# Linear attention's key sums on one core: two heads a product, four chunks a burst, and the denominators' sums by accumulating transfers

## The chip, the core and the metric

The kernel runs on one NeuronCore of a Trainium2 chip. The core has a matrix engine (TensorE, PE in the profile; its loads of stationary tiles are a row of their own, PEld), three elementwise engines (VectorE or DVE, ScalarE or ACT, GpSimd or POOL) and SyncE (SP), which issues most of the DMA transfers. The engines run their own instruction streams in order and wait for each other on semaphores. The metric is the device time of one execution in microseconds (us). Before the change it was 516.2 us, the median of three runs (515.8 to 516.62).

## What is computed

For 2048 tokens of width 512 the output is a gated mix of two layers, `g * a + (1 - g) * b`, with `g` the sigmoid of a dot product per token. `b` is a feed-forward layer of width 1792 with a squared ReLU. `a` is linear attention with 32 heads of 16 values each:

```python
pq = jnp.einsum("bhsd,hdf->bhsf", q, w_phi)
pk = jnp.einsum("bhsd,hdf->bhsf", k, w_phi)
phi_q = jnp.concatenate([_softmax(pq, axis=-1), _softmax(-pq, axis=-1)], axis=-1)
phi_k = jnp.concatenate([_softmax(pk, axis=-1), _softmax(-pk, axis=-1)], axis=-1)
kv = jnp.einsum("bhsf,bhsd->bhfd", phi_k, v)
z  = jnp.einsum("bhsf->bhf", phi_k)
num = jnp.einsum("bhqf,bhfd->bhqd", phi_q, kv)
den = jnp.einsum("bhqf,bhf->bhq", phi_q, z)[..., None] + 1e-6
o = num / den
```

All inputs are 32-bit floats. What the change touches are `kv`, for each head the sum over all tokens of the key features (32 numbers) times the values (16), and `z`, the sum over all tokens of the key features alone.

## The kernel before

**The feed-forward layer carries the order of the work.** A work list of 56 entries runs through two sweeps (one half of the 1792 hidden columns each), four blocks of 512 tokens and seven groups of 128 hidden columns. For each entry TensorE does 12 products "up" (into `u`) and 12 products "down" (into `d0` to `d3`); each 32-bit product is made of three, of high and low parts (`mm3`, lines 68 to 72). Between two entries stand slots: slot 2t comes ahead of entry t's up products and slot 2t+1 ahead of its down products. All attention work is placed by `at(slot, function, ...)` into these slots. The tile framework then orders each engine's instructions, with a priority for those under `tc.high_priority`.

**Keys and values** belong to the first sweep. The 16 chunks of 128 tokens follow each other 2.9 slots apart. `do_k` projects a chunk's keys into one bank of TensorE's accumulators, `exps` makes the two sets of exponentials from it (maxima, minima and two differences on DVE, lines 331 to 334; exponentials on ACT, line 336; sums and reciprocals on DVE), and `scaled` (line 345) multiplies them into the features `phi`, 1024 numbers per token. Two slots later `do_v` projects the values into the same single bank, and ACT copies them (line 517) into `vext`, whose rows have 17 numbers per head: 16 values and a one, written at the start by GpSimd. Five slots after the second of two chunks `do_kv` makes their products: for each head a stationary tile of 17 columns (values and the one) and 32 moving columns (the features), 32 products per chunk, 64 per burst, four different 32-column strips of the array one after the other (line 354). All chunks accumulate in one bank, `kvps`, in rows 32j to 32j+16 and 256 columns; row 16 of each strip holds `z`, because of the one.

**After the last chunk** (slot 53) `kv_done` copies the four strips to `kvs` (line 543), sends `z` through DRAM to all partitions (`zrow`, lines 546 and 549), transposes `kvs` on TensorE (`kvt`, line 554) and copies the result into `kvb`, which the numerators (`num`, line 400) use. GpSimd multiplies the query features with `z` (line 363).

**Beside that**, DVE folds the query weights with `w_phi` in 64 steps (`foldq_step`, line 236), each with a load of 256 KB (`wqr`, line 229, on SP's queue); after each 16 steps it transposes a quarter into `wqt`, and at slot 46 `foldq_move` writes all of it to DRAM (`wqm`) in four transfers and reads it back as the rows `wq`, which `foldq_ready` splits into high and low parts (`wqh`, `wql`).

Buffers are shared by tag: `e` and `ez` hold features (three in all), `phiT` is one large tile used in turn by several stages, `vz` holds `vext` and later `z`, `oh` and `ol` the numerators and until then the tokens of the gate (`gate_load`).

Of the kernel before, what the change touches and what calls it, by code (L numbers as in the profile page):

```python
# [26 lines left out]
VW = DH + 1  # L27
NV = 3
# [4 lines left out]
def tile_gated_mix(ctx: ExitStack, tc: tile.TileContext, xT, xn, wqT, wkT, wphi, wv, wo, w1, b1, w2, b2, gw, out):  # L33
# [110 lines left out]
    hold = pool("hold", NV)  # L144
# [15 lines left out]
    vext = [hold.tile([P, H * VW], F32, tag="vz", name=f"vext{i}") for i in range(NV)]  # L160
    heads = lambda v: v.rearrange("p (h v) -> p h v", v=VW)
    for v in vext:
        nc.gpsimd.memset(heads(v)[:, :, DH:VW], 1.0)
# [62 lines left out]
    def foldq_step(i):  # L226
# [10 lines left out]
        if e == DH - 1:  # L237
            if g == 0:
                st["wqt"] = work.tile([P, 2, 4, NG, 32], F32, tag="phiT", name="wqt", bufs=1).rearrange(
                    "p u r g s -> p (u r g s)").rearrange("p (c g j) -> p c g j", c=4 * NK, g=NK)  # L240
            nc.vector.transpose(st["wqt"][:, :, g, :], st["acc"].rearrange("p (c j) -> p c j", c=4 * NK))

    def foldq_move():
        for r in range(4):
            nc.sync.dma_start(wqm.rearrange("c i (r n) -> r i c n", r=4)[r],
                              st["wqt"][32 * r:32 * r + 32].rearrange("p c g j -> p c (g j)"))
        st["wq"] = [row() for _ in range(NK)]
        for k in range(NK):
            nc.sync.dma_start(st["wq"][k], wqm[4 * k:4 * k + 4].rearrange("c i n -> (c i) n"))
# [45 lines left out]
    def gate_load(n):  # L295
        t = st["xn", n] = work.tile([P, D], F32, tag="ol" if n % 2 else "oh", name="xn", bufs=2)
        nc.sync.dma_start(t, xn[n])
# [25 lines left out]
    def exps(ps, tag="e"):  # L323
# [4 lines left out]
        e = work.tile([P, H, 2, DH], F32, tag=tag, name="e", bufs=2 if tag == "e" else 1)  # L328
# [21 lines left out]
    def kv_chunk(n, kvps, phi, v):  # L350
        for i in range(NG):
            for j in range(4):
                h = 8 * (i % 4) + 4 * (i // 4) + j
                nc.tensor.matmul(kvps[32 * j:32 * j + VW, 32 * i:32 * i + 32], v[:, h * VW:(h + 1) * VW],
                                 phi[:, 32 * h:32 * h + 32],
                                 start=(n == 0 and i == 0), stop=(n == NB * NC - 1),
                                 skip_group_check=True)

# [149 lines left out]
    def do_k(b, c):  # L508

        n = b * NC + c  # L510
        e3, r = exps(project(c, st["x", b], st["wa"], "k"), "ez" if n % NV == NV - 1 else "e")
        st["phi", n] = scaled(e3, r, nc.vector)

    def do_v(b, n, c):
        ps = project(c, st["x", b], st["wb"], "v")
        with tc.high_priority(offset=AHEAD):
            nc.scalar.activation(heads(vext[n % NV])[:, :, :DH], ps.rearrange("p (h f) -> p h f", f=DH), AF.Copy)

    def do_kv(n):
        if n == 0:  # L520
            st["kv"] = ps_b.tile([P, 2 * P], F32, tag="s", name="kvps")
        for m in (n, n + 1):
            kv_chunk(m, st["kv"], st["phi", m], vext[m % NV])

# [12 lines left out]
    def kv_done():  # L537
        kvps, kvs = st["kv"], row()[:, :2 * P]
        nc.gpsimd.memset(kvs, 0.0)
        for j in range(4):  # L540
            s = slice(32 * j, 32 * j + VW)
            with tc.high_priority(offset=AHEAD):
                nc.vector.tensor_copy(kvs[s, :], kvps[s, :])
        zr = zrow.rearrange("(i q j f) -> q j i f", i=4, q=2, f=32)
        for q in range(2):
            nc.sync.dma_start(zr[q], kvs[DH::32, q * P:(q + 1) * P].rearrange("p (i f) -> p i f", f=32))
        for half in range(2):
            z = hold.tile([P, H * VW], F32, tag="vz", name=f"z{half}")[:, :D]
# [7 lines left out]
        for j in range(4):  # L556
            s = slice(32 * j, 32 * j + 32)
            with tc.high_priority(offset=AHEAD):
                nc.vector.tensor_copy(kvb[s, :, DH * (j % 2):DH * (j % 2 + 1)], kt[s, :, :DH])
# [35 lines left out]
    for b in range(NB):  # L595
        for c in range(NC):
            s = b * SL + 3 * c - 5 if b else 3
            at(s, gate_load, b * NC + c)
            at(s + 3 if b else 7 + c, gate_dot, b * NC + c)
# [139 lines left out]
```

## Time and profile before

| | |
|---|---|
| median of 3 runs | 516.2 us (515.8 to 516.62) |
| the profiled execution | 515.94 us |
| its span, first to last instruction | 514.2 us |
| PE busy | 509.1 us |
| DVE busy | 400.9 us |
| ACT busy | 227.0 us |
| POOL busy | 44.1 us |
| DMA | 75.35 MB, 147 GB/s on the mean |

A row of a group reads: line, engine, operation, output <- inputs (buffer numbers left out), shape and count, then times. A row of the timeline reads: start in us from the span's start, duration in us, engine, line, operation, count. A row of waits reads: who waited for whom, us in total, times, longest. PE's records of products overlap, because products are pipelined; the distance of their starts tells what one costs.

### The profile page before, as it was taken

To read this page: it belongs to the slowest core of one execution; us is meant where nothing else is said; L and a number is where in the kernel's file an instruction comes from. 1 tells how busy PE (TensorE), PEld (TensorE's weight loads), DVE (VectorE), ACT (ScalarE), POOL (GpSimd) and SP (SyncE) were. 2 spreads that over 40 slices of the span, in tenths; PEclk is the share of its full clock that TensorE was granted. 3 is DMA by queue.
4 is the path that set the end of the run, shared out by engine and by line. 5 is a ranking of instruction groups with operands and counts; after the bars stand their busy time and mean duration, and the time that the engine had idled before them with its cause. 6 is when DMAs were issued, how large, how long until landed. Compare 5 with 4: busy or idle time off the path is not lost.

```text
span 514.2 us, 9242 instructions
## 1 busy us (share of the span) xinstructions
PE 509.1 (99%) x3526; PEld 410.1 (80%) x3526; DVE 400.9 (78%) x680; ACT 227.0 (44%) x389; POOL 44.1 (9%) x44
## 2 busy tenths in 40 slices
PE   9999999999999999999999999999999999999997
PEld 4887888888888888888888878788787878788875
DVE  3769769796988798886889787988779677797723
ACT  5676253254224344253854544243625353343530
POOL 1000000000000000000003040301111111202100
PEclk9999999999999999999999999999999999999999
DMA  8997535467644477558359152213153321032102
GB/s 290 302 330 231 160 112 176 132 208 253 211 140 146 152 264 218 203 145 222 91 165 343 43 174 65 92 45 101 34 158 114 84 78 47 4 100 82 43 22 82
DMA packets 48421, 75.35 MB, mean 147 GB/s; under 512 B 7032, under 2 KB 15736, under 8 KB 48376
## 3 DMA queue, kind: packets, MB, share of 16 engines
q1 hardware_dynamic: 47912, 74.35, 45.8%
q8 instruction: 28, 0.46, 0.4%
q10 hardware_dynamic: 432, 0.39, 0.2%
q14 instruction: 17, 0.14, 0.1%
q0 software_dynamic: 32, 0.01, 0.0%
HBM read 50.60 MB, written 17.83 MB: 133 GB/s over the span
## 4 chain that ended last, share of the span: by engine, by line
PE 98%; ACT 1%; DVE 0%; DVEq 0%; issue 0%
PE u L70 10%; PE d L70 10%; PE u L72 10%; PE d L71 10%; PE d L72 10%; PE u L71 10%; PE v L70 3%; PE k L70 3%; PE k L71 3%; PE k L72 3%; PE q L72 3%; PE att L70 3%; PE q L70 3%; PE q L71 3%; PE att L71 3%; PE att L72 3%
## 5 line engine op out<-in xcount | busy, mean ns | idle before, releaser
L435 ACT ACTIVATE r<-u,b1c 128x512 f32<-128x512 f32 x56 | 38.6, 689 | 164.7 <-PE u L72 164.2
L70 PE MATMUL d<-w2h,hh 128*128 128x512 f32 x224 | 87.5, 391 | 0.0
L72 PE MATMUL d<-w2h,hl 128*128 128x512 f32 x224 | 87.3, 390 | 0.0
L71 PE MATMUL d<-w2l,hh 128*128 128x512 f32 x224 | 87.2, 389 | 0.0
L70 PE MATMUL u<-xh,w1h 128*128 128x512 f32 x220 | 86.6, 393 | 0.0
L72 PE MATMUL u<-xh,w1l 128*128 128x512 f32 x220 | 85.9, 390 | 0.0
L71 PE MATMUL u<-xl,w1h 128*128 128x512 f32 x220 | 85.7, 390 | 0.0
L65 DVE TENSOR_TENSOR hl<-r,hh 128x512 fp32r<-128x512 f32 x56 | 37.8, 675 | 35.5 <-ACT hh L62 35.5
L339 DVE TENSOR_REDUCE sm<-e 128x64 f32<-128x1024 f32 x32 | 38.9, 1216 | 28.2 <-ACT e L336 28.2
L363 POOL TENSOR_TENSOR ez<-e,z 128x512 f32<-128x512 f32 x32 | 42.0, 1332 | 217.6 <-ACT e L336 211.5
L70 PEld LDWEIGHTS u<-xh,w1h 128*128 128x128 f32 x220 | 41.3, 188 | 11.7 <-issue 2.1
L70 PEld LDWEIGHTS d<-w2h,hh 128*128 128x128 f32 x224 | 42.1, 188 | 9.3 <-issue 0.6
L72 PEld LDWEIGHTS d<-w2h,hl 128*128 128x128 f32 x224 | 42.1, 188 | 8.7
L71 PEld LDWEIGHTS d<-w2l,hh 128*128 128x128 f32 x224 | 42.1, 188 | 8.6
L72 PEld LDWEIGHTS u<-xh,w1l 128*128 128x128 f32 x220 | 41.3, 188 | 9.4 <-DVE w1l L65 0.8
L71 PEld LDWEIGHTS u<-xl,w1h 128*128 128x128 f32 x220 | 41.3, 188 | 8.3
L236 DVE SCALAR_TENSOR_TENSOR row<-wqr,phc,row 128x512 f32<-128x512 f32 x60 | 44.5, 741 | 3.9 <-DMA wqr<-in_wqT 3.5
L336 ACT ACTIVATE e<-e 128x1024 f32<-128x1024 f32 x32 | 33.8, 1057 | 22.7 <-DVE e L334 22.4
L387 ACT ACTIVATE phiT<-tb 32x256 f32<-32x256 f32 x64 | 26.4, 413 | 32.5 <-DVE tb L381 31.9
L62 ACT ACTIVATE hh<-r 128x512 fp32r<-128x512 f32 x56 | 35.3, 630 | 1.5
L436 ACT ACTIVATE r<-r 128x512 f32<-128x512 f32 x56 | 35.2, 628 | 1.1
L365 DVE TENSOR_REDUCE dz<-ez 128x64 f32<-128x1024 f32 x16 | 19.3, 1207 | 9.5 <-POOL ez L363 9.4
(102 smaller groups left out, 860.5 us busy)
## 6 DMA issues: line engine op xcount, KB each, us to landing
wqr<-in_wqT SPq DMA_DIRECT2D x64, 256.0 KB
in<-in_w SPq DMA_DIRECT2D x24, 256.0 KB
phiT<-tb SPq DMA_DIRECT2D x192, 32.0 KB
xin<-in_xT SPq DMA_DIRECT2D x16, 256.0 KB
xn<-in_xn SPq DMA_DIRECT2D x16, 256.0 KB
xkept<-xh SPq DMA_DIRECT2D x16, 256.0 KB
xkept<-xl SPq DMA_DIRECT2D x16, 256.0 KB
part<-row SPq DMA_DIRECT2D x16, 256.0 KB
```

Source lines behind the costliest of these rows:

```text
L62: i = nc.scalar.activation(hi, src, AF.Copy)
L65: st["low"] = elo.tensor_tensor(lo, src, hi.bitcast(F32), ALU.subtract)
L70: nc.tensor.matmul(o, ah[:, sa], bh[:, sb], start=first, stop=False)
L71: nc.tensor.matmul(o, ah[:, sa], bl[:, sb], start=False, stop=False)
L72: return nc.tensor.matmul(o, al[:, sa], bh[:, sb], start=False, stop=last)
L236: nc.vector.scalar_tensor_tensor(st["acc"], t, s, st["acc"], op0=ALU.mult, op1=ALU.add)
L336: nc.scalar.activation(ef, ef, AF.Exp)
L339: nc.vector.tensor_reduce(sm, e3, AX.X, ALU.add)
L363: nc.gpsimd.tensor_tensor(ez[:, hs, :], e3[:, hs, :], zbc[half], ALU.mult)
L387: nc.scalar.activation(dst, src, AF.Copy)
L435: nc.scalar.activation(r, ps, AF.Relu, bias=b1c[:, fc:fc + 1])
L436: nc.scalar.activation(r, r, AF.Square)
```

## The change

**Products.** The values are kept without the one, in 512 columns in another order (`val`), so that the values of two heads lie side by side as 32 columns. One product takes these as stationary tile and the features of the same two heads as 64 moving columns (two runs of 32). Of its result the two blocks on the diagonal are used; the other two are left alone. A chunk has 16 products in place of 32, and `do_kv` makes four chunks per burst in place of two: four bursts, in slots 18, 29, 41 and 53. Five buffers each for features and values replace three: two of the features' lie in `phiT` (`ebig`), two of the values' in the buffers of tag `ol`, so `gate_load` uses `oh` alone.

**The sums z.** GpSimd issues, after each of the first 15 chunks, a transfer of the features (128 x 1024 numbers) to `zacc` in DRAM, the first writing and the others adding to what stands there. SP loads the result (`zsum`) after chunk 15 has been scaled in the program's order. At the end of the last burst eight products with a stationary tile of ones (128 x 32) sum `zsum` and the features of chunk 15 over the partitions, into columns 256 to 511 of the same bank. `kv_done` copies the bank as a whole and sends one row of each strip to `zrow`.

**The folded query weights.** Each quarter is transposed into a row tile and written to `wqm` at once, in four transfers of 32 x 16 runs of 128 bytes; `wqt` is gone.

```diff
-NV = 3
+NV = 5
...
-    vext = [hold.tile([P, H * VW], F32, tag="vz", name=f"vext{i}") for i in range(NV)]
-    heads = lambda v: v.rearrange("p (h v) -> p h v", v=VW)
-    for v in vext:
-        nc.gpsimd.memset(heads(v)[:, :, DH:VW], 1.0)
+    zacc = dram.tile([P, 2 * D], F32, name="zacc")
+    val = [hold.tile([P, D], F32, tag="vz", name=f"val{i}") for i in range(3)]
+    val += [work.tile([P, D], F32, tag="ol", name=f"val{i}", bufs=2) for i in range(3, NV)]
...
-            nc.vector.transpose(st["wqt"][:, :, g, :], st["acc"].rearrange("p (c j) -> p c j", c=4 * NK))
...
+            t = row()
+            nc.vector.transpose(t, st["acc"])
+            for r in range(4):
+                nc.sync.dma_start(wqm.rearrange("c i (r g j) -> r g i c j", r=4, g=NK)[r, g],
+                                  t[32 * r:32 * r + 32].rearrange("p (c j) -> p c j", j=32))
...
     def kv_chunk(n, kvps, phi, v):
-        for i in range(NG):
+        ph = phi.rearrange("p (a g f) -> p a g f", a=4, f=2 * DH)
+        for i in range(4):
             for j in range(4):
-                h = 8 * (i % 4) + 4 * (i // 4) + j
-                nc.tensor.matmul(kvps[32 * j:32 * j + VW, 32 * i:32 * i + 32], v[:, h * VW:(h + 1) * VW],
-                                 phi[:, 32 * h:32 * h + 32],
+                m, g = i % 2, 4 * (i // 2) + j
+                nc.tensor.matmul(kvps[32 * j:32 * j + 32, 64 * i:64 * i + 64],
+                                 v[:, 64 * g + 32 * m:64 * g + 32 * m + 32], ph[:, 2 * m:2 * m + 2, g, :],
                                  start=(n == 0 and i == 0), stop=(n == NB * NC - 1),
                                  skip_group_check=True)
+    def z_keep(n):
+        nc.gpsimd.dma_start(zacc, st["phi", n], **({"accum_op": ALU.add} if n else {}))
+
+    def z_sum(kvps, parts):
+        one = nc.const_aps.tensor(1.0, (P, 32), F32)
+        for i, t in enumerate(parts):
+            for j in range(4):
+                nc.tensor.matmul(kvps[32 * j:32 * j + 32, 256:512], one, t[:, 256 * j:256 * j + 256],
+                                 start=i == 0, stop=i == len(parts) - 1, skip_group_check=True)
...
         st["phi", n] = scaled(e3, r, nc.vector)
+        if n < NB * NC - 1:
+            z_keep(n)
+        else:
+            st["z"] = work.tile([P, 2 * D], F32, tag="tb", name="zsum", bufs=2)
+            nc.sync.dma_start(st["z"], zacc)
...
-        for m in (n, n + 1):
-            kv_chunk(m, st["kv"], st["phi", m], vext[m % NV])
+        for m in range(n, n + 4):
+            kv_chunk(m, st["kv"], st["phi", m], val[m % NV])
+        if n == NB * NC - 4:
+            z_sum(st["kv"], (st["z"], st["phi", n + 3]))
...
-        kvps, kvs = st["kv"], row()[:, :2 * P]
-        nc.gpsimd.memset(kvs, 0.0)
-        for j in range(4):
-            s = slice(32 * j, 32 * j + VW)
-            with tc.high_priority(offset=AHEAD):
-                nc.vector.tensor_copy(kvs[s, :], kvps[s, :])
...
+        kvs = row()
+        with tc.high_priority(offset=AHEAD):
+            nc.vector.tensor_copy(kvs, st["kv"])
+        nc.sync.dma_start(zrow.rearrange("(j f) -> j f", j=4), kvs[::32, 256:512])
...
-            if c % 2:
-                at(s + 5, do_kv, n - 1)
+            if c == NC - 1:
+                at(s + 4.5, do_kv, n - 3)
```

How the instructions move is shown at three places. The first is TensorE's stream at the last burst, at the end of the first sweep; before the change:

```order
L354 MATMUL kvps<-e,vext_113 17x32 x32
L354 MATMUL kvps<-e,vext_111 17x32 x32
L70 MATMUL d_2491<-w2h_643,hh 128x512
L71 MATMUL d_2491<-w2l_644,hh 128x512
L72 MATMUL d_2491<-w2h_643,hl 128x512
L70 MATMUL d_2492<-w2h_643,hh 128x512
L71 MATMUL d_2492<-w2l_644,hh 128x512
L72 MATMUL d_2492<-w2h_643,hl 128x512
L70 MATMUL d_2493<-w2h_643,hh 128x512
L71 MATMUL d_2493<-w2l_644,hh 128x512
L554 MATMUL kvt<-ident,row 128x128 x2
```

And the same place after it, where line numbers are those of the changed file (L355 the products, L369 the ones, L580 the transposes):

```order
L355 MATMUL kvps<-e,val_114 32x64 x16
L355 MATMUL kvps<-ebig,val_115 32x64 x16
L355 MATMUL kvps<-ebig,val_116 32x64 x16
L355 MATMUL kvps<-e,val_112 32x64 x16
L369 MATMUL kvps<-zsum,const-float32-1.0 32x256 x4
L369 MATMUL kvps<-e,const-float32-1.0 32x256 x4
L69 MATMUL d_2323<-w2h_643,hh 128x512
L70 MATMUL d_2323<-w2l_644,hh 128x512
L71 MATMUL d_2323<-w2h_643,hl 128x512
L69 MATMUL d_2324<-w2h_643,hh 128x512
L580 MATMUL kvt<-ident,row 128x128 x2
```

The burst holds four chunks and the products of ones, and the transposes stand behind four products of the down group in place of eight.

The second is DVE's stream around the scaling of chunk 15 (the last row of each piece), with the splits of the folded query weights (`wql`); before:

```order
L339 TENSOR_REDUCE sm<-e 128x64
L65 TENSOR_TENSOR hl<-r,hh 128x512
L341 RECIPROCAL r<-sm 128x64
L303 SCALAR_TENSOR_TENSOR xn,lg<-xn,gwb 128x512
L345 TENSOR_TENSOR e<-e,r 128x1024
```

And after:

```order
L339 TENSOR_REDUCE sm<-e 128x64
L64 TENSOR_TENSOR wql_2633<-row,wqh_2632 128x512
L64 TENSOR_TENSOR wql_2675<-row,wqh_2674 128x512
L64 TENSOR_TENSOR wql_2691<-row,wqh_2690 128x512
L341 RECIPROCAL r<-sm 128x64
L64 TENSOR_TENSOR hl<-r,hh 128x512
L345 TENSOR_TENSOR e<-e,r 128x1024
```

Three splits, which stood behind the scaling, now stand ahead of it.

The third is DVE's stream at the copy of the finished sums; before:

```order
L65 TENSOR_TENSOR w2l_2932<-in,w2h_2931 128x512
L311 RECIPROCAL ge<-inv 128x1
L313 TENSOR_SCALAR eps<-inv 128x1
L65 TENSOR_TENSOR wol_3029<-in,woh_3028 128x512
L312 TENSOR_SCALAR rest<-ge 128x1
L543 COPY row<-kvps 17x256 x4
L65 TENSOR_TENSOR hl<-r,hh 128x512
L559 COPY kvb<-kvt 32x8x16 x4
```

And after:

```order
L64 TENSOR_TENSOR w2l_2703<-in,w2h_2702 128x512
L64 TENSOR_TENSOR wol_2808<-in,woh_2807 128x512
L64 TENSOR_TENSOR hl<-r,hh 128x512
L571 COPY row<-kvps 128x512
L64 TENSOR_TENSOR wol_2817<-in,woh_2816 128x512
L586 COPY kvb<-kvt 32x8x16 x4
```

The copy is one in place of four, and the split `hl` of the feed-forward layer moves from behind it to ahead of it.

On SP's queue the load of `zsum` stands behind the last four transfers to `wqm` and ahead of one load of `in` and the four loads `row<-wqm`; the first four loads of `x` for the second sweep move ahead of the loads of `wo`.

53 lines of the change are left out of this document (29 added, 24 removed).

## The prediction

> **What bounds the kernel now.** I read the page's busy row first, then the clock row, the chain that ended last and TensorE's waits.
>
> ```profile
> PE 509.1 (99%) x3526; PEld 410.1 (80%) x3526; DVE 400.9 (78%) x680; ACT 227.0 (44%) x389; POOL 44.1 (9%) x44
> PEclk9999999999999999999999999999999999999999
> PE 98%; ACT 1%; DVE 0%; DVEq 0%; issue 0%
> PE warm L467 <- DVE zeros L464: 1.2, 1, 1.2
> ```
>
> TensorE is busy for 99% of the span, its clock is granted in full, 98% of the chain lies on it, and its only listed wait is 1.2 us at the start. So the time is the sum of what TensorE spends from one product to the next. An edit counts in full if it changes that sum, and on other engines only if it makes TensorE wait.
>
> The sum has to be taken from starts, since busy times of overlapping products are unions. Here is TensorE's timeline around the first burst of keys-times-values products (`kvps`) and a normal stretch behind it; columns are start and duration in us.
>
> ```profile
> 61.08 0.39 PE L72 MATMUL d<-w2h,hl 128*128 128x512 f32 x1
> 61.40 1.27 PE L354 MATMUL kvps<-e,vext 128*17 128x32 f32 x128
> 62.59 0.50 PE L70 MATMUL v<-wvh,xh 128*128 128x512 f32 x1
> 65.44 0.39 PE L70 MATMUL u<-xh,w1h 128*128 128x512 f32 x1
> 68.16 0.39 PE L70 MATMUL k<-wkh,xh 128*128 128x512 f32 x1
> ```
>
> From 65.44 to 68.16 stand 12 ordinary products in 2.72 us: one per 0.2267. From 61.08 to 65.44 stand 13 such intervals (2.95) and the burst, 4.36 in all. **A burst costs 4.36 - 2.95 = 1.41 us.** How it splits shows in the counts of `kvps` records begun by 61.64, 61.90 and 62.40 (each 32-bit product leaves two records).
>
> ```profile
> L354 PE MATMUL kvps<-e,vext x32: 193/193/205, 61.4 to 61.6; 128*17 128x32 f32 x32
> L354 PE MATMUL kvps<-e,vext x60: 193/193/205, 61.4 to 61.9; 128*17 128x32 f32 x60
> L354 PE MATMUL kvps<-e,vext x120: 193/193/205, 61.4 to 62.4; 128*17 128x32 f32 x120
> L354 PE MATMUL kvps<-e,vext x1024: 190/193/207, 61.4 to 257.5; 128*17 128x32 f32 x171
> 256.38 1.32 PE L354 MATMUL kvps<-e,vext 128*17 128x32 f32 x128
> ```
>
> The first 32 come 7.5 ns apart (0.24 us), the rest 8.3 ns apart (60 in 0.50 us): 1.07 us for 128. The other 0.34 us is entering and leaving: the drain ahead of the burst and the slow products behind it. 1024 records are 8 bursts; the last is 0.05 longer (1.32 against 1.27). **All eight: 8 x 1.41 + 0.05 = 11.33 us.**
>
> **What a product of 64 columns takes.** The trace has none with a stationary tile of 32 columns over 128 rows. The nearest is `num` (32 columns stationary, 256 moving, eight tiles of the array abreast). These are its records begun by 304.73, 304.74, 305.16 and 305.17, and then the timeline.
>
> ```profile
> L400 PE MATMUL num<-phiT,kvb x8: 400/400/401, 304.5 to 304.5; 64*32 64x256 f32 x8
> L400 PE MATMUL num<-phiT,kvb x9: 376/400/401, 304.5 to 304.7; 64*32 64x256 f32 x9
> L400 PE MATMUL num<-phiT,kvb x24: 376/376/401, 304.5 to 305.0; 64*32 64x256 f32 x24
> L400 PE MATMUL num<-phiT,kvb x25: 376/376/401, 304.5 to 305.2; 64*32 64x256 f32 x25
> 304.18 0.39 PE L72 MATMUL d<-w2h,hl 128*128 128x512 f32 x1
> 304.50 1.09 PE L400 MATMUL num<-phiT,kvb 64*32 64x256 f32 x32
> 306.32 0.40 PE L70 MATMUL u<-xh,w1h 128*128 128x512 f32 x1
> ```
>
> Eight records start together and the next eight when these have passed: two groups in 0.43 us, 0.216 a group, 0.84 ns per column and tile. The moving side sets that pace. For 64 columns it gives 54 ns; `kvps` uses four tiles abreast, so 13.5 ns per record. The other end is twice the old pitch's first part, 15 ns, or twice its later part, 16.7. I take 14: the later 8.3 looks like a limit per instruction (a record brings a weight load and a product whatever its width), under which half as many records may each take 16.7 without feeling it.
>
> Four bursts of 128 records: 4 x (128 x 14 ns + 0.34) = 8.53 us, with ends 8.3 (13.5 ns) and 9.9 (16.7 ns). Against 11.33 this gains **2.80 us** (1.4 to 3.0).
>
> A rule would make it more. The Trainium skill, "TensorEngine Tiling (Array Packing)", Instruction Overhead, says that each matmul carries about 60 cycles of overhead, so that one column takes as long as 60; by it 64 columns would pass at almost the old 8.3 ns, and the gain would be 5.7 us in place of 2.8. The `num` rows speak against it at 256 columns, and no row here has 64; it stands among the rivals.
>
> **The products of ones** are new: eight at the end of the last burst, 256 columns each, 16 records, four abreast: 4 x 0.216 = 0.86 us. From 304.18 to 306.32 the `num` burst costs 2.14 less four intervals, 1.23, of which 0.86 are its four groups: 0.37 for entering and leaving, 0.03 more than the 0.34 already counted. Together **+0.89 us** (0.45 if eight could run abreast, 1.75 if two).
>
> **The accumulating transfers** (15, 512 KB each, on GpSimd's queue, each waiting for the one before) are shown by no row. GpSimd has nothing else queued behind them until the queries' products with `z`, so their price is lateness and DMA time.
>
> ```profile
> L345 DVE TENSOR_TENSOR e<-e,r x16: 1180/1217/1222, 38.7 to 247.4; 128x1024 f32<-128x1024 f32 x16
> q1 hardware_dynamic: 47912, 74.35, 45.8%
> b1c<-in_b POOLq DMA_DIRECT2D x1, 7.0 KB, 5.2
> 232.81 1.22 DVE L345 TENSOR_TENSOR e<-e,r 128x1024 f32<-128x1024 f32 x1
> 239.19 1.88 SPq L249 DMA_DIRECT2D row<-wqm  x4
> 260.87 0.39 PE L70 MATMUL q<-wqh,xh 128*128 128x512 f32 x1
> ```
>
> The features of a chunk are ready every (247.4 - 38.7) / 15 = 13.9 us. At the mean rate of q1 (45.8% of 514.2 us for 74.35 MB) 0.52 MB take 1.7 us; moved three times (read, read the sum, write) 5 us; GpSimd's one transfer needed 5.2 us to land with 7 KB. So my estimate lies between 1.7 and 10.3 us, under 13.9, and they do not pile up: 0 us. The skill's "DMA: Bandwidth & Descriptors", Anatomy of one DMA, fits 2.0 us plus bytes at 436 GB/s for this path, 3.2 us here; by it, too, nothing piles up.
>
> The load of the sums stands on SP's queue behind the last of them, and behind it wait `in` and the four `row<-wqm` loads of the queries' weights. The features of chunk 14 are ready at 234.0; with a transfer of 5 to 10 us the loads go out at about 242 to 247 instead of 239.2. The queries start at 260.87, 1.9 us earlier in the new program, and DVE now splits these weights ahead of scaling chunk 15. That scaling ends at 248.6 (247.4 + 1.22), and its burst starts at 256.38, 7.8 us later: three splits of 0.6 use 1.9, and 5.9 remain. A transfer up to about 12 us is covered; beyond that TensorE waits the excess.
>
> **The folding of the query weights** moves to 16 transfers of 128-byte runs from 4 of 512-byte runs, spread over 100 us, with the loads of `wqr` queued behind them on SP. Their cover is DVE's lead on TensorE, tightest in chunk 11.
>
> ```profile
> 186.58 0.67 DVE L334 TENSOR_TENSOR e<-mn,k 128x512 f32<-128x512 f32 x1
> 188.17 0.39 PE L70 MATMUL v<-wvh,xh 128*128 128x512 f32 x1
> DVE row L236 <- DMA wqr<-in_wqT: 3.5, 6, 1.0
> ```
>
> DVE frees the bank of `k` at 187.25, `v` takes it at 188.17: 0.9 us. Today DVE waits 3.5 us for `wqr` in 6 places, none of which reaches TensorE. With more DMA traffic I bound the new stalls between 0 and 3 us and take 0, since waits grow first where 2 to 4 us cover them.
>
> **The end of the sums** (kv_done): four copies become one, and the transposes `kvt` move up from behind eight products to behind four.
>
> ```profile
> 258.73 0.62 ACT L62 ACTIVATE hh<-r 128x512 fp32r<-128x512 f32 x1
> 257.82 1.72 DVE L543 COPY row<-kvps 17x256 f32<-17x256 f32 x4 [1.19 <-PE kvps L354]
> 259.58 0.69 DVE L65 TENSOR_TENSOR hl<-r,hh 128x512 fp32r<-128x512 f32 x1
> 259.69 0.41 PE L554 MATMUL kvt<-ident,row 128*128 128x128 f32 x2
> ```
>
> One copy of 128x512 takes about 0.7 us (as the `hl` row), 1.0 less than today, which is about what the four products fewer take away; but DVE now does `hl` first, which waits for ACT's `hh`. The last burst is longer by 1.6 us, so `hh` should be done by its end. Zero, at most 0.7 us. The larger load of the value copies, the new tiles for features and values, and the two gate buffers instead of four wait only for work several slots back: nothing.
>
> **Sum:** -2.80 + 0.89 = **-1.9 us**. The profiled execution took 515.94 us with a span of 514.2; that would be 514.0 and 512.3. The median shown is 516.2, 0.3 higher: **514.3 us**. One measurement of this kernel can tell about 0.2%, 1.0 us, from no change.
>
> **Rivals.**
> *The accumulating transfers pile up (slower).* Serial, each waiting for the last: from 39.9 (the first scaling's 38.7 and 1.2), 15 of length d end at 39.9 + 15d, and the sums must be read by about 255. It decides at d = 14 us. At 16 they end at 280, SP's queue and the last burst stand, and TensorE waits some 25 us: 539 us. For it: no row shows such a transfer, DMA is half busy. Against: it needs eight times the plain 1.7 us. Chance 0.08.
> *DVE comes late (no change).* The transfers and short runs delay `wqr`, DVE stands in front of the maxima of `k`, and `v` waits for the bank. With 2 us in all, 0.13 per chunk or a few of 0.5: 516.2. For it: the 0.9 us above. Against: 3.5 us of such waits cost nothing today. Chance 0.13.
> *The wider product takes twice the old later pitch* (16.7 ns, no gain per column): -1.4 + 0.9 = -0.5, 515.7 us, within the bound. Chance 0.06.
> *The count alone sets the time* (8.3 ns): -5.7 + 0.9 = -4.8, 511.4 us. Chance 0.05. The change then does more than the forecast; that its halving of the count brings nothing is the rival before.
>
> **How the numbers follow.** The forecast has 0.68; its own range is 513.2 (13.5 ns and ones at 0.45 give 513.6, less 0.4 for the scatter of the runs shown, 515.8 to 516.62) to 515.2 (1 us of small stalls). To hold 8 in 10 I go up to the second and third rival, 516.2 and a little scatter: **513.2 to 516.4**; the two outer ones, 0.13, and a little of the second, are left out. Faster by over 0.2%: 0.67 + 0.05 + 0.02 = 0.74. Within: 0.01 + 0.11 + 0.04 = 0.16. Slower: 0.08 + 0.02 = 0.10.
>
> **What would show it.** Right: four bursts, about 2.1 us each by the same sum of starts, the last near 3.0; records four at a time every 54 to 56 ns; `zacc` transfers landing within 10 us; no new wait of TensorE. Wrong: bursts of 1.4 us (count rules) or 2.5 us (16.7 ns); GpSimd's transfers back to back with no gap; a wait of TensorE's `v` for DVE, or of `kvps` for `zsum` or the scaling; `kvt` behind DVE's `hl`.

## The result and the profile after

The changed kernel takes **540.7 us** (median of 6 runs, 537.47 to 542.92) against 516.1 for the kernel before (6 runs, 515.76 to 516.83): ratio 1.047 [1.045, 1.050]. Forecast were 514.3 us and a range up to 516.4. The profiled execution took 542.42 us with a span of 540.6, 26.4 us more than before. The page of the changed kernel, the same rows as were shown of before, and the two DMA queues that carry the work (packets, MB, share of 16 engines' span):

```profile
PE 514.8 (95%) x3030; PEld 412.3 (76%) x3030; DVE 400.5 (74%) x677; ACT 227.3 (42%) x389; POOL 55.7 (10%) x55
PEclk9999999999799999999998999999999999999999
...
q1 hardware_dynamic: 54360, 74.87, 44.1%
q0 software_dynamic: 2192, 7.87, 8.5%
...
PE 68%; DMA 15%; DVE 11%; ACT 3%; issue 3%; SPq 0%; DVEq 0%; ACTq 0%
DMA wqr<-in_wqT 14%; PE d L70 7%; PE d L69 7%; PE d L71 7%; PE u L69 7%; PE u L71 7%; PE u L70 7%; PE q L71 3%; PE q L70 3%; PE att L70 3%; PE att L71 3%; PE att L69 3%; PE q L69 3%; DVE row L234 2%; PE num L413 2%
```

DVE has as much work as before (400.5 against 400.9 us), and TensorE is no longer the whole chain: its share went from 98% to 68%, and the largest single item is now a load, `wqr`, with 14%. The transfers to `zacc` are all but 0.01 MB of q0: 7.87 MB in 8.5% of the engines' time, where q1 moves 74.87 MB in 44.1%. Per byte that is 1.8 times as long.

First the part that was to gain. TensorE's timeline at the first burst and at the last, start and duration in us:

```profile
88.41 0.39 PE L71 MATMUL d<-w2h,hl 128*128 128x512 f32 x1
88.73 1.55 PE L355 MATMUL kvps<-e,val 128*32 128x64 f32 x96
90.09 0.63 PE L355 MATMUL kvps<-ebig,val 128*32 128x64 f32 x32
90.65 0.50 PE L69 MATMUL v<-wvh,xh 128*128 128x512 f32 x1
...
92.14 0.39 PE L69 MATMUL v<-wvh,xh 128*128 128x512 f32 x1
...
275.38 0.39 PE L71 MATMUL u<-xh,w1l 128*128 128x512 f32 x1
...
277.50 0.61 PE L369 MATMUL kvps<-zsum,const-float32-1.0 128*32 128x256 f32 x8
277.94 0.61 PE L369 MATMUL kvps<-e,const-float32-1.0 128*32 128x256 f32 x8
...
279.06 0.40 PE L71 MATMUL d<-w2h,hl 128*128 128x512 f32 x1
```

From 88.41 to 92.14 stand seven ordinary intervals (7 x 0.2267 = 1.59) and the burst: 3.73 - 1.59 = 2.14 us. From 275.38 to 279.06 stand three and the burst with the products of ones: 3.68 - 0.68 = 3.00. The two bursts between them cost 2.14 each by the same sum. Forecast were 8.53 / 4 = 2.13 and about 3.0. This part is as predicted to a few hundredths.

The loss stands in the waits: line, what it waited for, us in total, times, longest.

```profile
PE v L69 <- DVE e L334: 7.5, 3, 4.0
PE d L69 <- DVE row L716: 4.6, 1, 4.6
PE kvt L580 <- DVE row L571: 3.7, 1, 3.7
PE v L69 <- DVE ebig L334: 3.4, 2, 2.7
...
DVE row L234 <- DMA wqr<-in_wqT: 36.8, 20, 4.5
```

With two more rows, of 0.9 and 0.4, these are 20.5 us of TensorE's time, in nine places, eight of them behind DVE (the 0.9 is behind ACT); before there was none but the start. DVE's own wait for `wqr` grew from 3.5 to 36.8 us.

What happens in one of these places shows the timeline of the changed kernel from 124 to 140 us (SP's queue, GpSimd, DVE and TensorE, some rows left out):

```profile
124.58 0.64 SPq L227 DMA_DIRECT2D wqr<-in_wqT  x1
...
126.20 0.86 POOL L363 DMA_DIRECT2D zacc<-e  x1 [12.74 <-DVE eps L309]
...
126.50 4.22 SPq L227 DMA_DIRECT2D wqr<-in_wqT  x3
...
129.34 0.75 DVE L234 SCALAR_TENSOR_TENSOR row<-wqr,phc,row 128x512 f32<-128x512 f32 x1 [0.86 <-DMA wqr<-in_wqT]
...
134.06 0.39 PE L71 MATMUL u<-xh,w1l 128*128 128x512 f32 x1
...
135.18 0.75 DVE L234 SCALAR_TENSOR_TENSOR row<-wqr,phc,row 128x512 f32<-128x512 f32 x1 [4.48 <-DMA wqr<-in_wqT]
135.84 0.68 DVE L331 TENSOR_REDUCE mx<-k 128x32 f32<-128x512 f32 x1
...
137.64 0.68 DVE L334 TENSOR_TENSOR e<-mn,k 128x512 f32<-128x512 f32 x1
...
138.46 0.76 PE L69 MATMUL v<-wvh,xh 128*128 128x512 f32 x1 [4.01 <-DVE e L334]
139.03 0.63 PE L70 MATMUL v<-wvl,xh 128*128 128x512 f32 x1
139.45 0.63 PE L71 MATMUL v<-wvh,xl 128*128 128x512 f32 x1
139.88 0.63 PE L69 MATMUL v<-wvh,xh 128*128 128x512 f32 x1
```

Read it from the top. SP issues a load of `wqr` at 124.58; counted through, it is the 25th of 64, and the step at 135.18 is the 25th that needs one. GpSimd issues a transfer at 126.20, whose data move from 130.4 to 134.3 by the packet records of the trace. From 131 to 133 SP's queue then moves 45 GB/s, against some 195 in the four microseconds ahead of the transfer's data. So the load comes late though it was issued before the transfer; DVE, which works in order, stands 4.48 us in front of the step that needs it, and the maxima of `k` are queued behind that step; TensorE has the next `v` to do, whose bank is free only when DVE has read `k`, and waits 4.01 us. After the wait its products come 0.427 us apart, 139.03 to 139.88 in two steps, in place of 0.2267. The windows view (start and end, length, busy time and count of each engine, then granted clock, DMA share, GB/s) has the clock of that stretch:

```profile
140.00:144.00 4.00, 4.00 (x12) 3.14 (x11) 4.00 (x6) 1.51 (x4) 0.00 (x0) 0.56 0.79 289
```

0.56 of full speed is granted. So a wait of 4 us is paid about one and a half times: twelve products at 0.2 us more are 2.4. The same stands behind the two other waits of this length (4.6 and 3.7 us), and not behind those up to 2.7 us, where products follow at the ordinary pace. The Trainium skill, "TensorE: Matmul & The Clock Gate", Part 1, says that the array falls to half its clock after an idle window of about 3.4 us, with 426.7 ns from start to start at 512 columns; the 0.427 here agree.

The sum closes to about 1 us. From the starts of TensorE's products in the two traces, gaps over 0.7 us cost 21.9 us more than ordinary intervals after (0 before), and intervals of 0.3 to 0.7 us cost 9.9 us more, against 4.6 before: 27.2 in all. Span difference and forecast gain make 26.4 + 1.9 = 28.3.

### The profile page after: what moved, and what is told of

It is laid out like the page before. It is cut to its first block, busy times and chain, and to the rows that moved or that the text cites. A ratio compares the mean times of both kernels' runs of the same rounds, so it can differ in the third digit from the quotient of the medians.

```text
span 540.6 us, 8331 instructions
## 1 busy us (share of the span) xinstructions
PE 514.8 (95%) x3030; PEld 412.3 (76%) x3030; DVE 400.5 (74%) x677; ACT 227.3 (42%) x389; POOL 55.7 (10%) x55
## 3 DMA queue, kind: packets, MB, share of 16 engines
q1 hardware_dynamic: 54360, 74.87, 44.1%
q0 software_dynamic: 2192, 7.87, 8.5%
## 4 chain that ended last, share of the span: by engine, by line
PE 68%; DMA 15%; DVE 11%; ACT 3%; issue 3%; SPq 0%; DVEq 0%; ACTq 0%
DMA wqr<-in_wqT 14%; PE d L70 7%; PE d L69 7%; PE d L71 7%; PE u L69 7%; PE u L71 7%; PE u L70 7%; PE q L71 3%; PE q L70 3%; PE att L70 3%; PE att L71 3%; PE att L69 3%; PE q L69 3%; DVE row L234 2%; PE num L413 2%
## 5 line engine op out<-in xcount | busy, mean ns | idle before, releaser
L69 PE MATMUL d<-w2h,hh 128*128 128x512 f32 x224 | 88.9, 397 | 4.6 <-DVE row L716 4.6
L70 PE MATMUL d<-w2l,hh 128*128 128x512 f32 x224 | 88.6, 395 | 0.0
L234 DVE SCALAR_TENSOR_TENSOR row<-wqr,phc,row 128x512 f32<-128x512 f32 x60 | 44.7, 745 | 37.1 <-DMA wqr<-in_wqT 36.8
L339 DVE TENSOR_REDUCE sm<-e 128x64 f32<-128x1024 f32 x26 | 31.6, 1216 | 22.8 <-ACT e L336 22.8
L336 ACT ACTIVATE e<-e 128x1024 f32<-128x1024 f32 x26 | 27.5, 1058 | 34.8 <-DVE e L334 34.6
L400 ACT ACTIVATE phiT<-tb 32x256 f32<-32x256 f32 x64 | 26.5, 414 | 32.5 <-DVE tb L394 31.8
L69 PE MATMUL v<-wvh,xh 128*128 128x512 f32 x64 | 26.7, 417 | 11.3 <-DVE e L334 7.5
```

The lines of the kernel that those rows point to most:

```text
L69: nc.tensor.matmul(o, ah[:, sa], bh[:, sb], start=first, stop=False)
L70: nc.tensor.matmul(o, ah[:, sa], bl[:, sb], start=False, stop=False)
L234: nc.vector.scalar_tensor_tensor(st["acc"], t, s, st["acc"], op0=ALU.mult, op1=ALU.add)
L336: nc.scalar.activation(ef, ef, AF.Exp)
L339: nc.vector.tensor_reduce(sm, e3, AX.X, ALU.add)
L400: nc.scalar.activation(dst, src, AF.Copy)
```

## The experiments

Theory A: the transfers hold all DMA engines for some microseconds each, SP's loads behind them come late, DVE waits in lumps, TensorE waits for DVE, and the clock adds to it. Rivals: B, the 128-byte runs of the folded query weights on SP's queue are what delays the loads; C, the new order of the stream and the fewer buffers cost by themselves. "Wait for `wqr`" is DVE's, total and longest; "TensorE" adds up its listed waits without the 1.2 us at the start. Both are of the profiled execution, which for the plain transfers was the fastest of its four (525.3 us) and for `wqr` from 128 rows the slowest of its nine (522.6).

| run | time, us | ratio to before | wait for `wqr` | TensorE |
|---|---|---|---|---|
| before | 516.1 | | 3.5, 1.0 | 0 |
| changed | 540.7 | 1.047 [1.045, 1.050] | 36.8, 4.5 | 20.5 |
| one transfer | 515.3 | 0.999 [0.998, 1.000] | 11.1, 2.0 | 1.5 |
| before + short runs | 518.3 | 1.005 [1.003, 1.006] | 9.9, 2.2 | 2.5 |
| before + transfers | 531.9 | 1.032 [1.030, 1.035] | 27.9, 5.1 | 11.4 |
| plain transfers | 527.9 | 1.023 [1.019, 1.028] | 20.6, 3.8 | 8.4 |
| GpSimd adds | 525.1 | 1.017 [1.015, 1.020] | 7.7, 1.8 | 8.8 |
| 512-byte rows | 541.3 | 1.049 [1.047, 1.051] | 37.5, 4.5 | 19.1 |
| `wqr` from 128 rows | 520.1 | 1.007 [1.005, 1.010] | 2.9, 2.9 | 5.7 |
| every second transfer | 531.7 | 1.029 [1.026, 1.033] | 23.6, 5.2 | 11.2 |
| `zsum` by GpSimd | 535.2 | 1.037 [1.035, 1.039] | 33.5, 4.4 | 14.0 |
| both cures | 514.8 | 0.997 [0.996, 0.998] | 0.9, 0.9 | 1.5 |
| before + late DVE | 521.4 | 1.010 [1.008, 1.012] | 6.5, 1.9 | 4.3 |
| both cures, laid out | 514.5 | 0.997 [0.996, 0.998] | 2.5, 1.3 | 1.1 |

**One transfer.** All of the change, but `z_keep` for the first chunk alone:

```
-        if n < NB * NC - 1:
+        if n == 0:
             z_keep(n)
-        else:
+        elif n == NB * NC - 1:
```

> The changed kernel with only the first of its 15 transfers to zacc; the sums z are then those of chunks 0 and 15 alone. Theory A (each accumulating transfer holds all 16 DMA engines for 3 to 4 us, the wqr loads on SP's queue come late behind it, DVE waits for them ahead of the maxima of k, and TensorE waits for DVE): 514.2 us, between 513.4 and 515.2; DVE's wait for wqr falls from 36.8 to below 8 us, TensorE's listed waits from 21 to below 3 us. Theory B (the 128-byte runs of the folded query weights on SP's queue make wqr late): it stays above 530 us. Theory C (the new order of the streams and the fewer buffers make TensorE wait, whatever the DMA does): it stays above 530 us.

515.34 us. The order of the program, the buffers and the short runs are all in it, so B and C are out as main causes: 25 of the 26 us hang on 14 transfers. It is 1.1 us above A's point and just above A's range, and the wait for `wqr` is 11.1 us where A had below 8, most of it harmless.

**Short runs alone.** The kernel before, with the folded weights written a quarter at a time in 128-byte runs, as the change does:

```
-            nc.vector.transpose(st["wqt"][:, :, g, :], st["acc"].rearrange("p (c j) -> p c j", c=4 * NK))
+            t = row()
+            nc.vector.transpose(t, st["acc"])
+            for r in range(4):
+                nc.sync.dma_start(wqm.rearrange("c i (r g j) -> r g i c j", r=4, g=NK)[r, g],
+                                  t[32 * r:32 * r + 32].rearrange("p (c j) -> p c j", j=32))
```

> The kernel before with one part of the change alone: each quarter of the folded query weights is written at once in four transfers of 128-byte runs, in place of four transfers of 512-byte runs at the end. Theory A: 516.1 us, within 1 us. Theory B: over 528 us, with DVE waiting for wqr behind each quarter. Theory C: 516 us.

518.31 us: the short runs cost 2.3 us, more than the 1 us that A allowed, and far from B's 528.

**Transfers alone.** The kernel before, plus 15 accumulating transfers that nobody reads:

```
         st["phi", n] = scaled(e3, r, nc.vector)
+        if n < NB * NC - 1:
+            nc.gpsimd.dma_start(zacc, st["phi", n], **({"accum_op": ALU.add} if n else {}))
```

> The kernel before with 15 accumulating transfers of the features to DRAM added and nothing else changed; their result is not read. Theory A: 530 to 545 us, since the transfers alone carry the loss; DVE's wait for wqr rises from 3.5 to over 25 us. Theories B and C: 516 to 518 us.

531.89 us, with TensorE waiting 11.4 us in the same way: A's expectation. With the short runs that is 15.8 + 2.3 = 18.1 of the 24.6 + 1.9 = 26.5 us to be explained; some 8 were still open here.

**Plain transfers.** The changed kernel without the addition in the transfer:

```
-        nc.gpsimd.dma_start(zacc, st["phi", n], **({"accum_op": ALU.add} if n else {}))
+        nc.gpsimd.dma_start(zacc, st["phi", n])
```

> The changed kernel with plain transfers of the same features from the same queue in place of accumulating ones; z is then of chunks 14 and 15 alone. In the changed kernel a 4 KB packet of the accumulating queue took 383 ns on the mean, where a 2 KB packet of the plain queue took 100. Theory A: plain packets of 4 KB take about half as long, so a transfer holds the engines for under 2 us and the loss of 24 us falls below half: 515 to 526 us. Theories B and C, and a version of A in which any transfer of 512 KB on that queue is enough whatever it does: 536 to 543 us.

527.94 us, above A's range: a plain transfer of the same size harms half as much, and I had put its harm too low. The 536 to 543 of B, of C and of the version of A in which any transfer is enough are missed too. The row of its software queue stands against the 8.5% above:

```profile
q0 software_dynamic: 2192, 7.87, 3.9%
```

The same packets and bytes take 3.9% of 16 engines over 523.5 us, 327 engine-us for 15 transfers: 1.4 us of all 16 engines each. With the addition it is 8.5% over 540.6: 735 engine-us, 3.1 us of all engines each. This is the time that packets were under way, waiting for the other queue's packets perhaps included. DVE's wait for `wqr` goes the same way: over the run with one transfer, (20.6 - 11.1) / 14 = 0.7 us a transfer plain (in the fastest execution) and (36.8 - 11.1) / 14 = 1.8 with the addition.

**GpSimd adds.** No transfer; GpSimd adds the features on chip, bursts take three chunks:

```
-        nc.gpsimd.dma_start(zacc, st["phi", n], **({"accum_op": ALU.add} if n else {}))
+        if n == 0:
+            nc.gpsimd.tensor_copy(st["zacc"], st["phi", n])
+        else:
+            nc.gpsimd.tensor_tensor(st["zacc"], st["zacc"], st["phi", n], ALU.add)
```

> Keeps the wider products, but has no transfer to DRAM for the sums: GpSimd adds each chunk's key features into a tile of on-chip memory (the second half of the tile that held two more chunks' features), so a burst takes three chunks instead of four, the last one stands alone, and z_sum multiplies one tile by ones (4 products instead of 8). Nothing of the computation is left out. Theory A (the transfers hold the 16 DMA engines, SP's loads of wqr come late, DVE and then TensorE wait): the wait of DVE for wqr stays near the 11.1 us of the run with a single transfer, and the time is 514.0 to 516.5 us, ratio 0.996 to 1.001: products 16 x 2.12 = 33.9 against 45.3 us for eight bursts in the kernel before is what was already in the sum, less 0.5 for the ones, plus about 2.3 for the short runs. Rival C (the new order of the stream and the fewer buffers cost by themselves): with one buffer fewer it is 518 or more.

(The figures 33.9 and 45.3 in that expectation take a burst's cost for a chunk's; by the starts in this run's trace the six bursts with the ones cost 5 x 1.69 + 1.22 = 9.7 us, against 11.3 before.) 525.09 us: A's range is missed. C's 518 or more is met, but the trace shows another cause, so that this run says little on the fewer buffers. GpSimd's and DVE's groups, busy us and mean ns behind the bar, and then the same DVE steps with their shortest, median and longest ns:

```profile
L365 POOL TENSOR_TENSOR ebig<-ebig,e 128x1024 f32<-128x1024 f32 x11 | 29.4, 2674 | 135.3 <-DVE e L344 57.2 <-ACT val L544 26.9 <-DVE eps L308 26.8
...
L233 DVE SCALAR_TENSOR_TENSOR row<-wqr,phc,row 128x512 f32<-128x512 f32 x60 | 56.4, 940 | 8.4 <-DMA wqr<-in_wqT 7.7 <-DVE hl L64 0.3
L64 DVE TENSOR_TENSOR hl<-r,hh 128x512 fp32r<-128x512 f32 x56 | 43.4, 775 | 20.4 <-ACT hh L61 20.4
...
L233 DVE SCALAR_TENSOR_TENSOR row<-wqr,phc,row x60: 651/746/2775, 75.7 to 240.1; 128x512 f32<-128x512 f32 x60
```

The same DVE steps take 940 ns in place of 745 on the mean, and DVE's busy time goes from 400.5 to 428.5 us. The median is 746 all the same: six of the 60 steps, each under way during an addition of GpSimd, take 2.5 to 2.8 us, and the rest what they took before. So DVE is not slowed throughout; single instructions are held up for about 2 us each. `wqr` is on time (7.7), and yet TensorE waits 6.6 us for DVE and 2.2 for ACT. It is another way of making DVE late, with the same end.

**512-byte rows.** The transfers written as `p (c f)` with `f=128` on both sides.

> The changed kernel with each accumulating transfer written in rows of 512 bytes instead of 4096: the same bytes, eight times the packets. Theory A, with the two queues served packet by packet: SP's packets of 2048 bytes keep the larger share of each engine, wqr's wait falls from 36.8 us to 10 to 25, the time is 517 to 532. Rival (bytes read, added and written back are what holds the engines, or small packets cost the adder as much as large ones): wqr's wait stays at 35 or more and the time is 540 or more.

541.31 us, and this tells nothing: the software queue again shows 2192 packets and 7.87 MB, so the rows were joined again and the transfer was the same. Whether smaller packets would leave SP's loads more room stays open.

**`wqr` from 128 rows.** The transfers stay; the load reads 128 rows in place of 8 rows given 16 times:

```
-        nc.sync.dma_start(t, wqT.rearrange("(j e) g d -> g e j d", e=DH)[g, e].unsqueeze(1).to_broadcast([8, DH, D]))
+        nc.sync.dma_start(t, xn[i % (NB * NC)])
```

> The changed kernel, accumulating transfers included, but the 64 loads of wqr read 128 separate rows of xn (as many bytes, spread over all 16 DMA engines) in place of 8 rows of in_wqT, each repeated for 16 partitions, which use 8 of the 16 engines. The folded query weights come from the wrong numbers. Theory A: SP's queue now makes up its delay between two transfers at about twice the rate, DVE's wait for wqr falls from 36.8 us to under 12 and the time is 514.5 to 520. Rivals: the transfers harm through something other than wqr's loads (DVE's or TensorE's own pace, the order of the stream): 535 or more, whatever wqr waits; the loads are late because the transfers stop them altogether, not because they recover slowly: wait 25 to 37, time 530 to 541.

The query weights are then folded from other numbers; the bytes loaded and DVE's steps are the same. 520.13 us (517.05 to 522.56), 20.6 less than the changed kernel, with the median just above A's range, and DVE waits 2.9 us for `wqr`, once. So most of the transfers' harm does not reach DVE or TensorE directly; it goes through these loads, and what made the loads weak was their form. The windows view, first of the kernel before, at a place where four loads of `wqr` are on their way and nothing else (5 us x 199 GB/s are 1.0 MB), then of the last run below (rows separate), in a transfer and behind it; last two columns DMA share and GB/s:

```profile
213.00:218.00 5.00, 5.00 (x24) 4.14 (x23) 3.87 (x7) 2.82 (x4) 0.00 (x0) 1.00 0.54 199
```

```profile
206.00:208.00 2.00, 2.00 (x10) 1.68 (x9) 2.00 (x4) 0.00 (x0) 0.00 (x0) 1.00 1.03 228
209.00:215.00 6.00, 6.00 (x28) 4.99 (x27) 3.86 (x6) 2.66 (x4) 0.00 (x0) 1.00 1.03 391
```

With 8 rows given 16 times the queue moves 199 GB/s at a share of 0.54 and no more, though four loads are outstanding; with separate rows it goes, with the other writes and loads on it, at a share of 1.03 and 391 GB/s once the transfer (206 to 208) is through. The Trainium skill, "DMA: Bandwidth & Descriptors", Rules for kernel authors, says that an outermost dimension of size c below 16 confines a transfer to at most c engines; 8 of 16 fit the 0.54. The packet records agree: with nothing but these loads under way (before, 205 to 208 us) 7 to 10 packets are in flight at a time, in the last run (209 to 215) mostly 15 to 19, and a packet of 2048 bytes takes 84 ns in both (median). So it is half as many packets at once, and not slower ones from reading the same row again and again; which engines carry them the trace does not name.

These times also give an estimate of the harm. A packet of the accumulating transfer takes about 328 ns in 131 to 133. If an engine serves the two queues by turns, eight engines pass 8 x 2048 bytes of `wqr` in 328 + 84 ns, 40 GB/s; the 45 seen there are near it. That the engines take turns is argued from this, not shown.

**Every second transfer.** `z_keep(n)` for even `n` alone.

> The changed kernel with a transfer for every second chunk alone (chunks 0, 2, ... 14: 8 in place of 15, about 28 us apart in place of 14; the sums of the odd chunks but the last are left out). In the runs so far the time went up by about 1 us for each us that DVE waits for wqr beyond some 10 us. Theory A with a reserve that is refilled between transfers: wqr waits 10 to 20 us, time 514.5 to 521. Rival (each transfer costs the same, 26.4 us over 14): about 13 us over the run with one transfer, 526 to 530.

531.72 us, above both ranges: A's "reserve that is refilled in between" is refuted. DVE waits (23.6 - 11.1) / 7 = 1.8 us per transfer, as much as with twice as many. At 28 us apart a transfer costs no less than at 14. The time even lost 16.4 us over 7 more transfers than one, more than the rival's 13; the wait of `wqr` alone does not fix the time, since 23.6 us here and 27.9 in the run with transfers alone, which lacks the gain of 1.9, end within 0.2 us of each other.

**`zsum` by GpSimd.** What the run with `wqr` from 128 rows left over, 520.1 against 514.3, stood for the most part at one place: `kvt`, with 3.7 of 5.7 us. The chain of it in the changed kernel, timeline of SP's queue, ACT, DVE and TensorE, and ahead of it SP's wait and the loads of `in_wo` in the kernel before, where the last burst began at 256.38:

```profile
SPq L540 <- DMA zacc<-ebig: 6.2, 1, 6.2
```

```profile
249.22 8.37 SPq L286 DMA_DIRECT2D in<-in_wo  x16
```

```profile
275.15 8.69 SPq L282 DMA_DIRECT2D in<-in_wo  x16
275.69 0.65 PE L355 MATMUL kvps<-e,val 128*32 128x64 f32 x32
...
280.10 0.63 ACT L61 ACTIVATE woh<-in 128x512 fp32r<-128x512 f32 x1 [3.48 <-DMA in<-in_wo]
280.77 0.69 DVE L64 TENSOR_TENSOR wol<-in,woh 128x512 fp32r<-128x512 f32 x1 [2.77 <-ACT woh L61]
281.95 0.69 DVE L64 TENSOR_TENSOR hl<-r,hh 128x512 fp32r<-128x512 f32 x1 [0.49 <-ACT hh L61]
282.56 0.69 DVE L571 COPY row<-kvps 128x512 f32<-128x512 f32 x1
283.39 0.59 PE L580 MATMUL kvt<-ident,row 128*128 128x128 f32 x2 [3.69 <-DVE row L571]
```

SP stands 6.2 us at the load of the sums until the last transfer has landed; what is queued behind it, down to the loads of `in_wo`, goes out late: 0.5 us ahead of the last burst, where it was 7.2 before. On the way ACT waits 4.26 us for the rows of `wqm`, DVE's splits come late with it, and SP stands for a buffer that they free. Then ACT waits for `in_wo`, DVE's `wol` and `hl` for ACT, the copy of the sums stands behind both, and TensorE's transposes wait 3.7 us for the copy. The edit:

```
-            nc.sync.dma_start(st["z"], zacc)
+            nc.gpsimd.dma_start(st["z"], zacc)
```

> The changed kernel with the load of the sums (zsum) issued by GpSimd instead of SP; nothing left out. In the changed kernel SP stands 6.2 us at that load, until the last accumulating transfer has landed, and behind it on SP stand the four reads of wqm and the loads of in_wo; DVE's copy of the sums is queued behind a split of in_wo's tiles (wol) that comes late, and TensorE's kvt waits 3.7 us for the copy. Theory A with this second path (SP held at zsum): the kvt wait falls under 1 us, the half-pace products behind it go too, the time is 533.5 to 537, 4 to 7 us less than the changed kernel's 540.7. Rival (the kvt wait comes from DVE's earlier delay by wqr and only happens to stand there): the wait stays above 2 us and the time is 539 or more.

535.23 us, 5.5 less than the changed kernel, and no wait of `kvt` is left. A second path, as expected.

**Both cures.** `wqr` from 128 rows and `zsum` by GpSimd, all 15 transfers in place.

> Both cures at once: wqr's loads read 128 rows of xn over all 16 engines (the folded query weights come from the wrong numbers, as in the run with these loads alone) and zsum is loaded by GpSimd. All 15 accumulating transfers stay. Theory A: only the path over wqr and the path over zsum cost, so the time is that of the sum without new waits: 514.0 to 516.0 (the kernel before less 1.9, plus up to 2 for the short runs). Rival (the transfers cost something besides these two paths): 518 or more.

514.80 us. The 26 us of loss are gone with the transfers still running: these two paths carry all of it, and their gains add up (20.6 + 5.5 us).

**Late DVE.** The kernel before, with one more DVE instruction behind each of the 64 steps:

```
                 nc.vector.scalar_tensor_tensor(st["acc"], t, s, st["acc"], op0=ALU.mult, op1=ALU.add)
+            nc.vector.tensor_scalar(t, t, s, None, ALU.mult)
```

> The kernel before, with nothing of the change, and behind each of the 64 steps that use wqr one more DVE instruction on the same tile (its result is not used): about 64 x 0.48 to 0.6 = 31 to 38 us more DVE work in the same places where the changed kernel's DVE waited 33 us longer for wqr, and no further transfer. It also keeps each tile of wqr that much longer. Theory A (a late DVE is enough by itself): 526 to 542. Rival (DVE is idle for a quarter of the span, so work of this size finds room, and the transfers act on TensorE in another way): under 520.

521.36 us, between the two expectations. DVE's added group in that run:

```profile
L237 DVE TENSOR_SCALAR wqr<-wqr,phc 128x512 f32<-128x512 f32 x64 | 30.7, 479 | 0.5
```

30.7 us of lateness in pieces of 0.48 cost 5.3 us, with one wait of TensorE of 3.1; 33 us more of waiting for `wqr`, in pieces up to 4.5, cost some 20. So a late DVE is enough, but not at the same price: in the runs with the loads of `wqr` in their old form and no added work on DVE or GpSimd, the loss goes with the longest wait (1.0 to 2.2 us: up to 2.3 over the kernel before; 3.8 to 5.2: 11 and more). That lumps beyond DVE's lead are what counts is argued from this, not shown by itself.

**Both cures, laid out.** The whole computation: `zsum` by GpSimd, and the query weights laid out ahead of the launch with each row 16 times in DRAM:

```
-        nc.sync.dma_start(t, wqT.rearrange("(j e) g d -> g e j d", e=DH)[g, e].unsqueeze(1).to_broadcast([8, DH, D]))
+        nc.sync.dma_start(t, wqT[i])
```

> The changed kernel with the whole computation, as a candidate: zsum is loaded by GpSimd, and the query weights are laid out in DRAM ahead of the launch with each row already 16 times beside itself, so that a load of wqr reads 128 separate rows (as many bytes as before) and uses all 16 engines. All 15 accumulating transfers stay. Theory A: the time of the run with both cures, 514.0 to 515.5, ratio to the kernel before 0.995 to 0.999, no wait of TensorE over 1.5 us. Rival (that run was fast because its loads of xn repeated 16 tiles of 256 KB, which these 64 separate tiles do not): 517 or more, with DVE waiting for wqr again.

514.51 us (7 runs, 514.27 to 514.74) against 516.15, ratio 0.997 [0.996, 0.998]. TensorE's waits in this run, all of them:

```profile
PE warm L480 <- DVE zeros L477: 1.2, 1, 1.2
PE u L505 <- DMA win<-in_w: 0.6, 2, 0.4
PE v L69 <- DVE ebig L334: 0.3, 1, 0.3
PE u L69 <- ACT w1h L61: 0.2, 1, 0.2
```

This version beats both kernels, the first by only 0.3% (1.6 us), the changed one by 26 us; the price is 16 MB of query weights in DRAM in place of 1, laid out outside the measured time.

## Why the prediction was wrong

By its own steps:

- **TensorE bounds, an edit counts by what it changes from start to start.** Right of the kernel before, and it is how the loss was added up too.
- **Bursts, -2.80, and ones, +0.89.** Right: 2.14 and 3.00 us measured against 2.13 and about 3.0. Freed of the new waits the change gives 514.5 us; the forecast was 514.3. The two rivals about the pace of a product are out, and with them, for these products, the gain of 5.7 us that the prediction worked out from the Trainium skill's 60 cycles.
- **The transfers do not pile up: 0 us.** Right that they do not pile up: the trace lists 3.8, 7.3 and 9.3 us to landing (least, median, most), under the 13.9 between them, though all above the 3.2 us that the prediction took from the Trainium skill's fit. Wrong that this is their whole price. It asked when each transfer is done, and not what it holds meanwhile: 3.1 us of all 16 engines, 15 times.
- **"I bound the new stalls between 0 and 3 us and take 0, since waits grow first where 2 to 4 us cover them."** This is the step that failed. The listed waits are 20.5 us and the slow products behind them some 5 more. The bound came from the 3.5 us of waiting for `wqr` today, which cost nothing, as if more of it would come in pieces of the same size. It came in lumps: in the place shown one transfer kept SP's queue at a quarter of its rate for 2 us, and DVE waited 4.5 us at once, where its lead at the tightest place was 0.9.
- **"DMA is half busy"** stands only among the reasons for the rival of piling up, and was not asked of the loads of `wqr`. For these a share of 0.54 was the full rate, 199 GB/s; there was little left with which to make up a delay. With separate rows of the same bytes the queue reaches 391 GB/s, and the wait falls to 2.9 us.
- **"A transfer up to about 12 us is covered"**, at the sums' load. The reads of the query weights were followed, the loads of `in_wo` further down the same queue were not, nor who waits for them: 5.5 us. (The times 242 to 247 there are some 3 us more than 234.0 and a transfer of 5 to 10 us; nothing else rests on them.)
- **"`hl` should be done by its end. Zero, at most 0.7."** 3.7 us: ACT stood 3.48 us at the split of `in_wo`, with `hh` behind it, and on DVE `wol` stood ahead of `hl`, so both and then the copy came late.
- **Short runs, in the same bound.** 2.3 us when added to the kernel before by themselves; with good loads they cost nothing that can be seen.
- **The rival "DVE comes late"** had the mechanism, place and victims right (transfers delay `wqr`, DVE stands in front of the maxima of `k`, `v` waits for the bank), with 2 us in all and 0.13. It was mis-sized by about ten times (20.6 us by this path), so that it stood as "no change" where it should have been the slower side. The rival that was put there, transfers one behind the other, did not happen; that its 539 us lie near the measured 540.7 is chance.
- **The clock** was in no step: after its three longest waits (3.7 to 4.6 us) TensorE runs at half pace for six to eleven products, so that part of such a wait is paid twice.

What stays open: the exact price of a lump as a function of DVE's lead (8 transfers cost 16.4 us more than one, 15 cost 25.4), what smaller packets would do, and what the fewer buffers of the run in which GpSimd adds cost.

## What to carry to other kernels

A DMA share of one half is no reserve until it is known what share the loads on which others wait can reach at all; here they were at their full rate with 0.54, and a change of their form took away 20 us. Price a new transfer not only by its landing but by the engine time it takes from the loads beside it, those already queued included, and compare the lump that gives, not only the sum, with the lead of the engine that waits. A load that waits for a chain of transfers belongs on a queue where nothing else stands behind it.

## What the runs showed of the hardware

- An accumulating transfer of 512 KB took 3.1 us of all 16 DMA engines, the plain one of the same packets 1.4; by landing they differ less (median 7.3 and 5.5 us).
- While such a transfer runs, the total rate falls at a share of about 1: to 228 GB/s at 1.03 in the last run (206 to 208), and to 130 at 1.01 in the slowest stretch looked at in the changed kernel, against 391 at 1.03 for separate rows without one.

```profile
80.50:82.50 2.00, 2.00 (x10) 1.67 (x9) 2.00 (x6) 0.00 (x0) 0.00 (x0) 1.00 1.01 130
```

- GpSimd's additions of 128x1024 (2.7 us each) held up single two-input steps of DVE: six of 60 took 2.5 to 2.8 us, the median stayed at 746 ns, and the mean rose from 745 to 940.
